# Seven block products for the first 1024 features of the last z2 projection

## The chip, the cores and the metric

The kernel is one program on 1 core of one Trainium2 chip. The metric is the device time of one execution in microseconds (us), with the inputs in HBM at the start and the output there at the end; several executions give a median. A core has five instruction streams that wait for each other only by semaphores. PE does matrix products from the on-chip memory SBUF into the accumulator memory PSUM, DVE and POOL do elementwise work, ACT does functions and scaled copies, and SP issues transfers (ACT and POOL issue some too).

## The reference, cut to what matters

```python
def reference(A_x, A_wqkv, A_wo, B_x, B_w_in, B_w_sp, B_b_sp, B_w_out):   # bf16, S = 2048, D = 1024, Fh = 1792
    x = A_x
    h = x + A(layernorm(x))        # attention, 32 heads, 8 keys at distance 2, then @ wo
    z = gelu(layernorm(h) @ w_in)  # 2048 x 3584, tanh form
    z1 = z[:, :Fh]
    z2 = layernorm(z[:, Fh:])      # over the 1792 features
    g = w_sp @ z2 + b_sp[:, None]  # over the 2048 tokens
    return h + (z1 * g) @ w_out
```

What the change touches is the product layernorm(h) @ w_in for the z2 half: the last 512 of the 2048 tokens, the first 1024 of the 1792 features.

## The kernel before

Tokens go through attention and the two projections in four chunks of 512 (CH), each of four tiles of 128. For a chunk, `head` multiplies by wo, adds x, stores h, takes the moments, normalises (`nrm`) and transposes each tile by a transfer that SP issues into hnT. `b_z2` then makes z2 with tokens as output rows, `b_z1` makes z1 with features as output rows. w_in lies in SBUF as four tiles: win0 and win1 for z2 (1024 and 768 columns), win2 and win3 for z1 (1024 and 768). After the last chunk a second phase multiplies by w_sp and w_out.

The last chunk (number 3) is treated apart. `b_z2(3)` is plain: for each tile 16 matmuls of 512 columns with win0, then 8 times 512 and 256 columns with win1, a gelu on ACT for each part, a square sum of 1792, statistics of that one tile, `nrm` on DVE and a store to HBM that POOL issues. `b_z1_blocks(3)` follows with seven block products (Strassen's form as Winograd has it): the 1024 long sum is cut in two halves, and so are the features and the tokens; sums of weight blocks (S, called form and win in the profile) and of token blocks (T, hnf) are formed on DVE in fp16, and seven products stand for eight. For range, the weights are scaled by a power of two, the level, which a chain over ACT, DVE and PE finds (`w1_level`: ACT takes absolute sums of win2 and win3). Its features come as three groups by blocks and two 128-feature pieces whole (`whole`, L1004) between the second group and the third.

A group of products uses two PSUM tiles of two banks, X and Y. X gets products 1, 7 and on top of them 2, 4; Y gets 5, 6 and on top 3:

```python
PRODS = (("k1", 1, 0), ("k4", 7, 0), ("k3", 5, 0), ("k2", 6, 0), ("k1", 2, 1), ("k4", 4, 1), ("k3", 3, 1))
```

ACT copies products 1, 7 and 5 into an SBUF tile of four slots (L1056, tile hb) before 2, 4 and 3 are added to their banks. DVE makes u = 6 + 1 (L1063), POOL w = 7 + 5 (L1064), DVE then c21, c22 and c12 in PSUM (L1065 to L1067), and ACT's gelu reads X and Y (L1083) and writes a tile of the pool xn, from which a transfer stores z1. PSUM tiles come from three slots "acc" of two banks; two more banks, "banka", opened at the end of attention, serve Y of the second group.

The order on each engine is fixed beforehand. All of this is recorded in an `Order`: each operation has an engine, an estimated time, what it depends on and how late, a priority, and slots that it takes or frees. `Order.run` then lists the operations in the order that a simple clock gives:

```python
def add(self, eng, us, fn, deps=(), prio=5.0, lat=0.1, take=None, free=None, table=None):
```

Each engine runs its list strictly in order, and an instruction that waits holds all behind it. Semaphores are set by the tile framework from the tiles that instructions read and write.

At the end of the stage the second phase begins: rows of w_sp (rawa, rawb) come by transposing transfers, DVE scales them by row (L1178) and makes their S forms (`t_forms`: L1190, L1196, L1192, L1194) and the z2 forms (`z_form`, L1214), PE runs `one_of` and `row_two` (L1279). z2 is loaded back from HBM by tokens: the halves (n, 0) of chunks 0 and 1, then (n, 1) of chunks 2 and 3 (L1205). `bias_rows` (L1168) multiplies a bias into the row scales, on DVE.

## Time and profile before

| | |
|---|---|
| median of 3 runs | 687.51 us (686.81 to 687.57) |
| profiled execution | 687.27 us |
| span of the profile | 685.5 us |
| PE busy | 679.0 us, 99% |
| DVE busy | 593.0 us, 87% |
| ACT busy | 357.6 us, 52% |
| POOL busy | 167.8 us, 24% |
| z2 of the last chunk on PE | 380.5 to 404.6 us |
| z1 of the last chunk on PE | 404.75 to 426.5 us |

The span runs from the first to the last instruction; the execution's own time has 1.8 us more around it. A line of a timeline gives start, length, engine, line of the kernel, operation, tiles out<-in and shape; in brackets is the idle time before it and what ended it. Lines of one kind that follow each other are joined, with their count at the end. Matmuls overlap, so a joined line of PE ends some 0.17 later than the next one starts. "Idle" counts only where nothing runs, so a wait on PE shows as a gap between lines.

### The profile page before, as it was taken

To read this page: it belongs to the slowest core of one execution; us is meant where nothing else is said; L and a number is where in the kernel's file an instruction comes from. 1 tells how busy PE (TensorE), PEld (TensorE's weight loads), DVE (VectorE), ACT (ScalarE), POOL (GpSimd) and SP (SyncE) were. 2 spreads that over 40 slices of the span, in tenths; PEclk is the share of its full clock that TensorE was granted. 3 is DMA by queue.
4 is the path that set the end of the run, shared out by engine and by line. 5 is a ranking of instruction groups with operands and counts; after the bars stand their busy time and mean duration, and the time that the engine had idled before them with its cause. 6 is when DMAs were issued, how large, how long until landed. Compare 5 with 4: busy or idle time off the path is not lost.

```text
span 685.5 us, 9209 instructions
## 1 busy us (share of the span) xinstructions
PE 679.0 (99%) x3424; PEld 360.4 (53%) x3441; DVE 593.0 (87%) x759; ACT 357.6 (52%) x530; POOL 167.8 (24%) x147
## 2 busy tenths in 40 slices
PE   9999999999999999999999999999999999999997
PEld 7766666566645445444544467444444444444443
DVE  6899899998999989999897868999799999755575
ACT  4547652353239998773883566388761122323131
POOL 0100010010210101000030124475461216553342
PEclk9999999999999999999999999999999999999999
DMA  8979579667995469444484996899957314642031
GB/s 319 335 242 248 169 192 280 154 160 262 226 350 226 93 239 238 163 176 118 111 220 135 199 295 186 284 285 317 275 184 190 123 53 132 185 123 93 1 122 63
DMA packets 144077, 133.07 MB, mean 194 GB/s; under 512 B 68768, under 2 KB 115776, under 8 KB 143904
## 3 DMA queue, kind: packets, MB, share of 16 engines
q1 hardware_dynamic: 132864, 88.93, 45.3%
q0 software_dynamic: 8416, 34.80, 17.9%
q10 hardware_dynamic: 2752, 8.75, 3.8%
q8 instruction: 27, 0.44, 0.3%
q14 instruction: 18, 0.15, 0.1%
HBM read 75.25 MB, written 33.10 MB: 158 GB/s over the span
## 4 chain that ended last, share of the span: by engine, by line
PE 99%; issue 0%; DVE 0%; ACT 0%; DVEq 0%
PE bank L1279 27%; PE acc L468 22%; PE acc L800 14%; PE acc L868 11%; PE banka L1279 10%; PE acc L723 8%; PE acc L1040 2%; PE acc L310 2%; PE wps L232 1%; PE acc L1004 1%; PE banka L1040 0%; PE L L562 0%; PE pb L624 0%; PE tpt L306 0%; ACT xnT L307 0%
## 5 line engine op out<-in xcount | busy, mean ns | idle before, releaser
L800 PE MATMUL acc<-win,hnT 128*128 128x512 bf16 (+1 forms) x501 | 97.4, 352 | 0.6
L800 PEld LDWEIGHTS <-hnT 128*128 128x128 bf16 x512 | 49.9, 98 | 47.4 <-issue 0.7
L532 DVE TENSOR_TENSOR prod<-qT,kT 128x4096 bf16<-128x4096 bf16 x32 | 72.7, 2282 | 1.6 <-ACT kT L474 1.3
L868 PE MATMUL acc<-hnT,win 128*128 128x512 bf16 x336 | 73.7, 379 | 0.0
L1279 PEld LDWEIGHTS <-zs 128*128 128x128 f16 x448 | 43.6, 98 | 52.8 <-DVE zs L1214 0.5
L479 ACT CAST stg<-acc 128x1024 bf16<-128x1024 f32 x36 | 36.4, 1011 | 61.9 <-PE acc L468 50.2
L468 PE MATMUL acc<-xnT,wk 128*128 128x512 bf16 x256 | 56.5, 379 | 0.0
L468 PE MATMUL acc<-xnT,wv 128*128 128x512 bf16 x256 | 56.4, 380 | 0.0
L723 PE MATMUL acc<-wo_sb,av_oT 128*128 128x512 bf16 x250 | 55.8, 379 | 0.3
L868 PEld LDWEIGHTS <-win 128*128 128x128 bf16 x336 | 32.7, 98 | 39.5 <-issue 0.7
L1279 PEld LDWEIGHTS <-z 128*128 128x128 bf16 x336 | 32.7, 98 | 39.1
L1279 PE MATMUL bank<-rawb,zs 128*128 128x512 f16 x224 | 52.6, 379 | 0.0
L1279 PE MATMUL banka<-rawa,z 128*128 128x512 f16 x224 | 51.9, 379 | 0.0
L1279 PE MATMUL bank<-form,zs 128*128 128x512 f16 x224 | 50.8, 379 | 0.0
L468 PEld LDWEIGHTS <-wk 128*128 128x128 bf16 x256 | 36.5, 143 | 19.0 <-issue 0.8
L468 PEld LDWEIGHTS <-wv 128*128 128x128 bf16 x256 | 36.5, 144 | 18.6 <-issue 0.5
L468 PE MATMUL acc<-xnT,wq 128*128 128x512 bf16 x192 | 41.9, 379 | 0.0
L723 PEld LDWEIGHTS <-av_oT 128*128 128x128 bf16 x256 | 24.9, 98 | 29.8
L807 ACT ACTIVATE u<-acc 128x1024 bf16<-128x1024 f32 (+1 forms) x32 | 29.2, 911 | 19.6 <-PE acc L800 19.4
L536 DVE TENSOR_TENSOR prod<-prod 128x2048 bf16<-128x2048 bf16 x32 | 38.7, 1216 | 0.0
L1279 PEld LDWEIGHTS <-sf 128*128 128x128 f16 x231 | 22.4, 98 | 26.3
L468 PEld LDWEIGHTS <-wq 128*128 128x128 bf16 x192 | 27.5, 143 | 13.9
(326 smaller groups left out, 1239.0 us busy)
## 6 DMA issues: line engine op xcount, KB each, us to landing
z<-z_d SPq DMA_DIRECT2D x28, 512.0 KB, 5.1
qkv_d<-stg SPq DMA_DIRECT2D x36, 256.0 KB, 4.7
wn<-in_B_w_sp_dram ACTq DMA_DIRECT2D x16, 512.0 KB, 5.5
z1c<-z_d SPq DMA_DIRECT2D x14, 512.0 KB, 4.8
z_d<-z1s SPq DMA_DIRECT2D x21, 256.0 KB, 2.8
z_d<-u SPq DMA_DIRECT2D x12, 448.0 KB, 2.5
av_y<-av_z POOLq DMA_DIRECT2D x4, 1024.0 KB, 9.8
av_oT<-av_zz POOLq DMA_DIRECT2D x4, 1024.0 KB, 15.3
```

The source lines that it names most:

```text
L232: T.matmul(wps[:], warm[:, 0:P], warm[:], start=True, stop=True)
L310: T.matmul(dst.rearrange("p (a b) -> p a b", b=P), wqs[:, kt, dl, :], xnT[0][:, lo:hi, kt, :], start=start, stop=stop)
L468: T.matmul(G[key][:, j, :].rearrange("p (a b) -> p a b", a=TPC), wv[:, kt, dl, :], xnT[c][:, :, kt, :], start=(kt == 0), stop=(kt == KT - 1))
L479: A.copy(stg[:], G[key][:])
L532: V.tensor_tensor(st["prod"][:], qT[:], kT[:, :, o:o + CH], op=ALU.mult)
L536: V.tensor_tensor(dst, p_[:, 0:4, :], p_[:, 4:8, :], op=ALU.add)
L723: T.matmul(st["acc", il][:, nh, :], oTs[c][:, dl, il * P:(il + 1) * P], wo_sb[:, dl, nh * CH:(nh + 1) * CH], start=(dl == 0), stop=(dl == ...
L800: T.matmul(accf[:, n0:n1], hnTs[c][:, il, kt, :], wins[hf][:, kt, n0:n1], start=(kt == 0), stop=(kt == KT - 1))
L807: A.activation(st["u", il][:, hf * 1024:hf * 1024 + wd], G["accz", c, il, hf][:].rearrange("p a b -> p (a b)")[:, 0:wd], ACTF.Gelu_apprx_t ...
L868: T.matmul(G["accy", c, fp][:, j, :].rearrange("p (a b) -> p a b", a=TPC), wt[:, kt, f0 * P:(f0 + 1) * P], hnTs[c][:, :, kt, :], start=(kt ...
L1040: T.matmul(d_, wt, mv, start=(not again and j == 0 and kt == 0), stop=(j == len(fps) - 1 and kt == 3), skip_group_check=bool(again))
L1279: T.matmul(dst, wts(k), mov(k), start=(first and k == 0), stop=(k == last - 1), skip_group_check=not first)
```

## The change

The z2 projection of the last chunk is made by `b_z2_blocks` in place of `b_z2`.

- The 768 columns of win1 stay whole (`late`), one tile after the other, ahead of the rest.
- The 1024 columns of win0 are made by seven products for each pair of tiles (0 and 2, 1 and 3), each of four matmuls of 512 columns. The order on PE is late 0, late 1, product 1 of both pairs, late 2, product 2 of both pairs, late 3, then 7, 5, 6, 4, 3 of the first pair and the same of the second. Y of the first pair uses the banka banks, all else acc tiles.
- The token forms are made once (`hn_forms`) and shared with z1. The weight forms of win0 are new: two of 2048 elements a partition, one in a tail behind win1 and one in place, and four of 1024 in xn tiles, with dependences that put them behind `nrm` or the moments of certain tiles.
- win0 is scaled on DVE, win2 and win3 now by 16 copies on ACT instead of four DVE operations. The level takes win0 into its sums, in 14 pieces of up to 1792, and is found during the last chunk's attention.
- The square sums are split in 768 and 1024, and the statistics of z2 are taken by pairs.
- In z1, Y of group 0 uses the banka banks instead of Y of group 1, and POOL makes its c22 into a zs tile. `bias_rows(0)` moves to POOL, the forms of the second phase change their order, and rawa is scaled tile by tile.
- On SP, the last z1 store of chunk 2 comes ahead of the h store of tile 2 and the transpose of that tile, and four z1 stores instead of three come ahead of chunk 2's transposes.

```diff
-                n_ = add("DVE", 0.5, nrm, [rs], prio=0.6)
+                n_ = G["normed2", il] = add("DVE", 0.5, nrm, [rs], prio=0.6)
+                G["moments2", il] = rs.deps[0][0]
...
+    def hn_forms(c):
+        ops, prev = {}, []
+        for m in (3, 1, 2, 4):
+            def f(m=m):
+                if "T" not in G:
+                    G["T"] = bp.tile([P, 4, 4, 2 * P], FP16, name="hnf", tag="hn%d" % ((c - 1) % 2), bufs=1)
...
+            prev = [add("DVE", 0.7, f, [G["hnT", c]] + prev, prio=2.65)]
+            ops[m] = prev[0]
+        return ops
+
+    def copies_tile():
+        if "copies" not in G:
+            G["copies"] = bp.tile([P, 4, CH], FP32, name="hb", tag="hb", bufs=1)
+        return G["copies"]
+
+    def b_z2_blocks(c, level):
+        st = {}
+        blk = lambda hk, j: w16(0)[:, 4 * hk:4 * hk + 4, j * CH:(j + 1) * CH]
+        scaled = []
+        for hk in range(2):
+            def sc(hk=hk):
+                half = wins[0][:, 4 * hk:4 * hk + 4, :]
+                V.tensor_scalar(half.bitcast(FP16), half, lev[:, 2:3], None, op0=ALU.mult)
+            scaled.append(add("DVE", 1.25, sc, [level, G["z2mm", c - 1, 0], G["avdone", c]], prio=2.6))
+
+        def s_half(m, h):
+            if m == 3:
+                return blk(0, 1)[:, 2 * h:2 * h + 2]
+            if m == 1:
+                return G["tail"].bitcast(FP16).rearrange("p (k n) -> p k n", k=4)[:, 2 * h:2 * h + 2]
+            if ("S", m, h) not in st:
+                st["S", m, h] = l1.tile([P, 2, CH], BF16, name="z1s", tag="xn", bufs=4)
+            return st["S", m, h][:].bitcast(FP16)
+
+        def s_w(m, h):
+            def f():
...
+            return f
+
+        sf_, prev = {}, []
+        for m, h in ((1, None), (3, None), (2, 0), (2, 1), (4, 0), (4, 1)):
+            behind = [] if h is None else [G["moments2" if h else "normed2", m // 2 - 1 + h]]
+            prev = [add("DVE", 1.22 if h is None else 0.7, s_w(m, h), scaled + behind + prev, prio=2.62, take="xn" if m in (2, 4) else None)]
+            sf_[m] = prev[0]
+        tf_ = G["tforms"] = hn_forms(c)
...
+        line = []
+
+        def late(il):
+            wd = win_specs[1][1]
+            deps = [G["hnT", c, il], G["win", 1]] + [(o, 0.0) for o in line[-1:]]
...
+                m_ = add("PE", 0.650, mm, deps, prio=order(), take="acc" if part == 0 else None)
+                deps = [(m_, 0.0)]
+            line.append(m_)
...
+            evs[il].append(add("ACT", 1.0, ev, [m_, G["z2st", c - 1, il]], prio=2.0, free="acc", lat=0.25, table="gelu"))
+            square(il, 1024, FH)
+
+        def bankof(a, b_):
+            nm = "XXYY"[b_]
+            if (nm, a) == ("Y", 0):
+                if (nm, a, b_) not in st:
+                    st[nm, a, b_] = zpools["ps"].tile([P, CH], FP32, name="banka", tag="banka", bufs=2)
+                return st[nm, a, b_][:]
+            if (nm, a) not in st:
+                st[nm, a] = new_acc()
+            return st[nm, a][:, b_ % 2, :]
+
+        def slot(a, n):
+            if n == 0:
+                if ("p1", a) not in st:
+                    st["p1", a] = zpools["z"].tile([P, CH], FP32, name="zs", tag="zs", bufs=5)
+                return st["p1", a][:]
+            return copies_tile()[:, n, :]
+
+        PR = {1: 0, 2: 0, 7: 1, 4: 1, 5: 2, 3: 2, 6: 3}
+        pe, cps = {}, {}
+        before = {}
+
+        def prod(p_, a):
+            def mm():
...
+            deps = scaled + [G["hnT", c, a + 2 if p_ == 3 else a]]
+            deps += [sf_[{3: 4, 5: 1, 6: 2, 7: 3}[p_]]] if p_ in (3, 5, 6, 7) else []
+            deps += [tf_[{7: 3, 5: 1, 6: 2, 4: 4}[p_]]] if p_ in (4, 5, 6, 7) else []
+            deps += [cps[{2: 1, 4: 7, 3: 5}[p_], a]] if p_ in (2, 3, 4) else []
+            deps += [G["close"]] + [(o, 0.0) for o in line[-1:]]
+            m_ = pe[p_, a] = add("PE", 0.864, mm, deps, prio=order(), take="acc" if p_ == 1 or (p_ == 5 and a == 1) else None)
+            line.append(m_)
+            if p_ in (1, 7, 5):
+                def cp():
+                    A.copy(slot(a, PR[p_]), bankof(a, PR[p_]))
+                cps[p_, a] = add("ACT", 0.6, cp, [m_] + ([G["hnT", c]] if a == 0 and p_ != 1 else []) + ([before[p_]] if a and p_ != 1 else []), prio=1.5, lat=0.15)
+
+        late(0)
+        late(1)
+        prod(1, 0)
+        prod(1, 1)
+        late(2)
+        prod(2, 0)
+        prod(2, 1)
+        late(3)
+        for a in range(2):
+            for p_ in (7, 5, 6, 4, 3):
+                prod(p_, a)
+
+            def dv(fn, deps, eng="DVE", us=0.7):
+                return add(eng, us, fn, deps, prio=2.0, lat=0.15)
+            u_ = dv(lambda a=a: V.tensor_tensor(slot(a, 3), bankof(a, 3), slot(a, 0), op=ALU.add), [pe[6, a], cps[1, a]] + ([before[7]] if a else []))
+            w_ = dv(lambda a=a: nc.gpsimd.tensor_tensor(slot(a, 1), slot(a, 1), slot(a, 2), op=ALU.add), [cps[7, a], cps[5, a]], eng="POOL", us=1.26)
+            c21 = dv(lambda a=a: V.tensor_tensor(bankof(a, 1), bankof(a, 1), slot(a, 3), op=ALU.add), [pe[4, a], u_])
+            c12 = dv(lambda a=a: V.tensor_tensor(bankof(a, 2), bankof(a, 2), slot(a, 3), op=ALU.add), [pe[3, a], u_])
+            if a == 0:
+                c22 = dv(lambda: nc.gpsimd.tensor_tensor(copies_tile()[:, 0, :], slot(0, 1), slot(0, 3), op=ALU.add), [u_, w_], eng="POOL", us=1.26)
+            else:
+                c22 = dv(lambda a=a: V.tensor_tensor(bankof(a, 3), slot(a, 1), slot(a, 3), op=ALU.add), [u_, w_, pe[3, a]])
+            before = {7: c22, 5: w_}
+            for il, nm, deps in ((a, "X", [pe[2, a], c21]), (a + 2, "Y", [c12, c22])):
+                halves = 2 if (nm, a) == ("Y", 0) else 1
+                for h_ in range(halves):
...
+                    evs[il].append(add("ACT", 1.22 if halves == 1 else 0.8, ev, [deps[h_]] if halves == 2 else deps, prio=1.9,
+                                       free="acc" if halves == 1 else None, lat=0.25, table="gelu"))
+                square(il, 0, 1024)
...
+            s0 = add("DVE", 0.32 if a else 0.48, st_tot, sqd[a] + sqd[a + 2], prio=0.5)
+            rs = batch_rstd(("l3", c, a), lambda cols=cols: st["stot"][:, cols], lambda cols=cols: st["sqs"][:, cols, 0],
+                            FH, f"l2_{a}", [s0], 0.5, cols=2)
+            for j in range(2):
...
+                n_ = add("DVE", 0.75, nrm, [rs], prio=0.6)
+                G["z2st", c, a + 2 * j] = dma_op(3.0, lambda: None, [n_])
+                G["z2n", c, a + 2 * j] = n_
 
...
-    W1CUTS = [(k, a) for k, n in ((2, 8), (3, 6)) for a in range(n)]
+    W1CUTS = [(k, a, min(a + FH, n)) for k, n in ((2, 8 * D), (3, 6 * D), (0, 8 * D)) for a in range(0, n, FH)]
...
         for k in (2, 3):
-            for hk in range(2):
-                def sc(k=k, hk=hk):
-                    half = wins[k][:, 4 * hk:4 * hk + 4, :]
-                    V.tensor_scalar(half.bitcast(FP16), half, lev[:, 2:3], None, op0=ALU.mult)
-                scaled[k, hk] = add("DVE", 1.5 if k == 2 else 1.15, sc, [level, last_mm[k], G["avdone", c]], prio=2.7)
-        hn = lambda hk, s2: hnTs[c][:, 2 * s2:2 * s2 + 2, 4 * hk:4 * hk + 4, :].rearrange("p il k s -> p k il s")
+            for kt in range(KT):
+                def sc(k=k, kt=kt):
+                    A.activation(w16(k)[:, kt, :], wins[k][:, kt, :], ACTF.Copy, scale=lev[:, 2:3])
+                scaled[k, kt // 4] = add("ACT", 1.06 if k == 2 else 0.81, sc, [level, last_mm[k]] + ([scaled[k, kt // 4]] if kt % 4 else []), prio=5.6)
...
-            prev = [add("DVE", 1.2, s_w(m, 2), [scaled[2, 0], scaled[2, 1], G["close"]] + prev, prio=2.8)]
+            behind = {1: G["normed2", 2], 3: G["moments2", 3], 2: G["normed2", 3], 4: G["normed2", 3]}[m]
+            prev = [add("DVE", 1.2, s_w(m, 2), [scaled[2, 0], scaled[2, 1], G["close"], behind] + prev, prio=2.8)]
...
-        before = {}
-        late = []
+        before = dict(G["copiesfree"])
+        before[1], before["c22"] = before[5], before[7]
...
-            if (nm, g) == ("Y", 1):
+            if (nm, g) == ("Y", 0):
...
-            c22 = dv("c22", lambda pt=pt, Y=Y: V.tensor_tensor(Y(1), pt(1), pt(3), op=ALU.add), [u_, w_, ops[3]])
+            if g == 0:
+                def apart(pt=pt):
+                    st["c22"] = zpools["z"].tile([P, CH], FP32, name="zs", tag="zs", bufs=5)
+                    nc.gpsimd.tensor_tensor(st["c22"][:], pt(1), pt(3), op=ALU.add)
+                c22 = dv("c22", apart, [u_, w_], eng="POOL", us=1.26)
+            else:
+                c22 = dv("c22", lambda pt=pt, Y=Y: V.tensor_tensor(Y(1), pt(1), pt(3), op=ALU.add), [u_, w_, ops[3]])
             c12 = dv("c12", lambda pt=pt, Y=Y: V.tensor_tensor(Y(0), Y(0), pt(3), op=ALU.add), [ops[3], u_])
...
-        V.tensor_tensor(wt_["rows"][:, cols], wt_["rows"][:, cols], wt_["b", pr], op=ALU.mult)
+        (V if pr else nc.gpsimd).tensor_tensor(wt_["rows"][:, cols], wt_["rows"][:, cols], wt_["b", pr], op=ALU.mult)
...
-    for c, r_ in ((0, r0_), (1, r1_)):
-        for k0 in range(0, NT, 4):
-            prev = [add("DVE", 1.2, lambda c=c, k0=k0: scale_raw(c, k0, 4), [r_, rl_] + prev, prio=3.5)]
-            if (c, k0) == (0, 4):
-                sc0 = prev[0]
+    for il, r_ in enumerate((ra_, rb_, r0_, r0_)):
+        prev = [add("DVE", 1.2, lambda il=il: scale_tile(0, il), [r_, rl_] + prev, prio=3.5)]
+    sc0 = prev[0]
+    for k0 in range(0, NT, 4):
+        prev = [add("DVE", 1.2, lambda k0=k0: scale_raw(1, k0, 4), [r1_] + prev, prio=3.5)]
     z_ld = {}
     for n in range(2):
         for hf in range(2):
             z_ld[n, hf] = dma_op(6.0, lambda n=n, hf=hf: load_z2f(n, hf), [r1_] + [G["z2st", 2 * hf + c, il] for c in range(2) for il in range(TPC)])
-    prev = [add("DVE", 0.7, lambda: bias_rows(0), prev, prio=3.55)]
+    add("POOL", 2.0, lambda: bias_rows(0), [rl_, G["hnT", NCH - 1]], prio=3.55)
     prev = [add("DVE", 0.7, lambda: z_form(0, 3), [z_ld[0, 0]] + prev, prio=3.55)]
-    for kind, n in (("z", 1), ("t", 0), ("t", 3), ("z", 2), ("z", 4), ("t", 1), ("t", 2)):
+    for kind, n in (("t", 0), ("z", 1), ("t", 3), ("z", 2), ("z", 4), ("t", 1), ("t", 2)):
```

183 lines of the change are left out of this document (121 added, 62 removed).

## The prediction

> **What bounds the kernel now.** I read the page first (busy time, then the chain that ended last), then the timelines of PE, ACT, DVE, POOL and SP's DMA queue between 370 and 445 us, where the changed stage lies, then the tile hnT.
>
> ```profile
> span 685.5 us, 9209 instructions
> PE 679.0 (99%) x3424; PEld 360.4 (53%) x3441; DVE 593.0 (87%) x759; ACT 357.6 (52%) x530; POOL 167.8 (24%) x147
> ...
> PE 99%; issue 0%; DVE 0%; ACT 0%; DVEq 0%
> ```
>
> PE is the bound, and the chain is all PE: a matmul less is its time less, and every wait put ahead of a matmul is time more. The PE timeline of the stage (start, length, line, tiles, count):
>
> ```profile
> 406.50 1.91 PE L1040 MATMUL acc<-hnf,form 128*128 128x256 f16 x16
> 408.24 1.04 PE L1040 MATMUL acc<-hnT,win 128*128 128x256 bf16 x8
> ...
> 416.98 3.62 PE L1004 MATMUL acc<-hnT,win 128*128 128x512 bf16 x16
> 420.43 1.04 PE L1040 MATMUL acc<-hnT,win 128*128 128x256 bf16 x8
> ...
> 440.36 1.89 PE L1279 MATMUL bank<-form,z 128*128 128x512 f16 x8
> ```
>
> Sixteen 512-column matmuls take 420.43 - 416.98 = 3.45 us, 0.216 each. A product of the block form takes four times that, 0.864 (eight of 256 columns in z1: 0.87). A group runs its products as 1, 7, 5, 6, 2, 4, 3; the first line holds 5 and 6, the second is 2. ACT copies 1, 7 and 5 out of PSUM:
>
> ```profile
> 406.69 1.07 ACT L1056 COPY hb<-acc 128x512 f32<-128x512 f32 x2 [0.85 <-PE acc L1040]
> 408.44 0.58 ACT L1056 COPY hb<-acc 128x512 f32<-128x512 f32 x1 [0.67 <-PE acc L1040]
> ...
> 413.77 0.60 ACT L1056 COPY hb<-banka 128x512 f32<-128x512 f32 x1
> 414.24 1.14 ACT L1083 ACTIVATE z1s<-acc,wlim 128x1024 bf16<-128x1024 f32 x1
> ...
> 422.38 1.07 ACT L1056 COPY hb<-acc 128x512 f32<-128x512 f32 x2 [0.49 <-PE acc L1040]
> ```
>
> The copies of 1 and 7 begin 0.19 after 7 ended (406.50), not after 1: two banks in one acc tile are waited for together. So does the copy of 5, 0.20 after 6 ended (408.24). The first pair is done at 407.76, product 2 begins at 408.24: 0.48 to spare, 0.42 behind the 0.06 of a semaphore. The third group: 423.45 against 423.92. The sum u that follows is DVE's:
>
> ```profile
> 409.06 0.69 DVE L1063 TENSOR_TENSOR hb<-acc,hb 128x512 f32<-128x512 f32 x1 [2.94 <-ACT hb L1056]
> ...
> 425.35 1.25 DVE L1214 TENSOR_TENSOR zs<-z,z 128x1024 f16<-128x1024 bf16 x1
> ...
> 436.63 2.29 DVE L1194 TENSOR_TENSOR form<-rawa,form 128x4096 f16<-128x4096 f16 x1
> ```
>
> ```profile
> 424.79 1.26 POOL L1064 TENSOR_TENSOR hb<-hb 128x512 f32<-128x512 f32 x1 [1.91 <-ACT hb L1056]
> ...
> 437.82 2.22 POOL L1523 TENSOR_TENSOR p<-p,p 128x512 f32<-128x512 f32 x1 [5.17 <-ACT p L1489]
> ```
>
> A DVE sum of two SBUF tiles takes 0.69 alone; begun inside a POOL sum it ends 0.55 after that (426.60 against 426.05). A POOL sum begun inside a DVE one (437.82) grows from 1.26 to 2.22 instead. Whichever starts first runs, the other waits. Last, the transposes of the tokens:
>
> ```profile
> 381.93 0.37 SPq L876 DMA_DIRECT2D z_d<-z1s  x1
> ...
> 386.67 1.26 SPq L752 DMA_TRANSPOSE hnT<-hb  x1
> ```
>
> ```profile
> L800 PE MATMUL acc<-win,hnT x126: 272/379/379, 380.5 to 404.6; 128*128 128x512 bf16 x94, 128*128 128x256 bf16 x32
> ...
> DMA to landing us min/median/max: 3.1/3.7/4.4
> ```
>
> The fourth transpose is issued at 386.67 and lands at 390.8. PE first needs that tile at 398.7: eight us of cover.
>
> **The change part by part.** Times are this profile's; the stage begins at 380.54 on PE.
>
> *Matmuls.* 64 of 512 columns become 56: 8 x 0.216 = **-1.73**. The 768-column part is the same work.
>
> *Fourth token tile.* PE now needs it after three whole tiles (2.59 each) and four products: 380.54 + 7.78 + 3.46 = 391.78, seven us sooner. Its transpose waits for nrm of tile 3, which on DVE now stands behind the last S form of win0 and a form of win2. That S form takes the xn buffer that the z1 store of 381.93 reads; the store lands in 4.0, at 385.9. Then 0.1 + 0.6 (pitch of a 1024 form) + 1.13 (2048 form) + 0.54 (nrm) + 0.1: issue at 388.4, landing after 3.1 to 4.4, that is 391.5 to 392.8. Wait 0 to 1.0; I take the 4.14 that this transpose took: **+0.75**.
>
> *Products of the second pair (tiles 1 and 3).* The order is 7, 5, 6, 4, 3, and 5 and 6 share an acc tile that 3 writes. From the end of 6: 0.20, the copy 0.62, u 0.69, 0.06 = 1.57 until 3 may start. One product (0.864) stands between, not two as in z1: **+0.70**. Pair one has its own bank for each, and no wait. Bounds 0 (copies by bank) to 0.8.
>
> *ACT order in z1.* In group 0 a gelu of the second pair now stands between the copies of 1 and 7, in group 2 a gelu of z1. Each has a pitch of 1.02 against 0.42 to spare: **+0.60 twice**. Bounds 0 and 1.0: the gelu's whole pitch, if the cover is gone.
>
> *Whole features after group 1.* Their acc tile comes free with group 0's gelu. Before it ACT now runs the copy of 5 and a square of 1024 (1.05 + 0.19, pitch about 1.08, by Abs): from the end of 6, 0.20 + 0.49 + 1.08 + 1.12 + 0.06 = 2.95 against three products, 2.6: **+0.35**, from 0 to 0.6.
>
> *Forms for the next stage (DVE).* Before, the last of them ends at 438.92 for the matmul at 440.36. After u of group 2 a rawb scaling (1.22, two SBUF inputs) replaces a form of 0.69, +0.52, and two more z forms follow, 1.2 together. That exceeds the 1.38 to spare by 0.35, but the +0.60 in group 2 falls behind u, ahead of the consumer, and covers it. What decides is L1523: before it started 1.2 after this form; now the form starts some 0.1 after the POOL sum would, and then waits for it: 0 or 0.95, **+0.5** as I can't place 0.1. Were the memory's bandwidth shared, both orders would stretch the form, and the sum would take 0.95; but its row of 2.29 beside POOL is not stretched. The Trainium skill, page "SBUF — State Buffer", section "SBUF: two separate sides", calls it an exclusive lock of the port pair of DVE and POOL, held by whichever starts first; by it the sum below is +1.3 or +2.3, never between, and the trace's two orders agree. Its "Perfetto Trace Analysis", section "Optimizing Scalar/DVE Operations", says that moving work between those two might not help; for the bias rows below, that is a warning against the move.
>
> *At nothing.* Bias rows to POOL: no POOL row of 128x1024 16-bit exists; 1.26 (its 512 float sum) to 2.5. Begun just ahead of the token forms it holds them up to 1.8, but they have the 2.59 of the fourth whole tile as cover. W sums and c22 on POOL: DVE's combining reads PSUM and isn't held. Level sums of 8192 more elements a partition, 8.5 us of ACT in attention 3: ACT idles more than that there and PE waits for none of it. Scaling win2 and win3, moved from DVE (4.6 us) to ACT (16 copies, about 15 us by L1419's 2.00 for 2048): behind the gelus they end near 399.5, the forms of win3 follow, and u of the second pair still comes later by its copy than by them. Scaling and forms of win0 (7.6 us of DVE) fill DVE's idle time from 374 to 391. SP: the z1(2) store goes ahead of h_d and the third transpose, which lands about 387 for 387.5; the extra store ahead of hnT(2)'s transposes costs 1.7 us of some 3 to spare. Statistics by pairs: z2 lands later, next paragraph.
>
> *Sum.* -1.73 + 0.75 + 0.70 + 1.20 + 0.35 + 0.5 = **+1.8**. The profiled execution took 687.27 (685.5 of span, 1.8 around it) and so becomes 689.1. It lies 0.24 below the median of the three runs, 687.51: **689.3**.
>
> **Rivals.**
> - *By bank.* If a copy went by its own bank, products 2 and 3 would not wait: terms 0.70 and 1.20 go, and the rest is 0 or so, 687.4: not slower. It decides if copies start at the end of 1 and 5. Against it: 406.69 and 408.44 above. Shorter landings end in the same place (the fourth tile at 3.1 and no POOL lock take 1.25 off, 688.0).
> - *Full gain.* All waits hidden, -1.73: 685.8. PE at 99% speaks for it, and so does the skill's "Perfetto Trace Analysis", section "Identifying Performance Opportunities": improve the most-contended engine. By it the sum would stop at the first term. Against it: the margins of 0.42 on which the old order ran.
> - *z2 late.* The last two z2 tiles are normed together at about 419 and stored by 420.5, two issues of 0.6 to 0.75 on. Before, such stores took 2.8 to 7.3 and the second pair of loads 4.7 and 6.0, landing at 421 and 423 for matmuls at 430.0 and 431.7, which the sum moves 1.3 later. Now the loads land at 428 to 432.6 and 429.7 to 434.3 for 431.3 and 433.0. The middle fits; the far end costs 1.3 more: 690.6.
>
> **How the numbers follow.** Forecast 0.54 (688.4 to 690.2 by its own bounds), by bank or shorter landings 0.26, full gain 0.10, z2 late 0.10. Two tenths of a per cent, 1.4 us, is about what a measurement tells from no change: 686.1 to 688.9. Full gain is the only case faster: 0.10. Slower: z2 late and four fifths of the forecast, 0.10 + 0.43 = 0.53. Same: the rest, 0.37. The range leaves out the full gain and ends a little outside the others: 687.0 to 690.9.
>
> **What would show it.** 56 matmuls and the 1.73; PE idle ahead of the fourth tile's first matmul, released by a hnT transpose issued near 388.4; ahead of product 3 of the second pair, released by DVE's u; ahead of product 2 of groups 0 and 2, released by an ACT copy with a gelu before it; ahead of the whole features; and at the matmul of L1194's form, with that form at 3.3 if the lock took it. Without these idles the forecast is wrong and the time is near 686; with an idle at the second z2 load it is above 690.

## The result, and the profile after

| | before | after |
|---|---|---|
| median | 687.52 us (6 runs, 686.81 to 687.78) | 691.28 us (6 runs, 691.12 to 691.41) |
| ratio to before, 95% interval | | 1.0056 [1.0043, 1.0069] |
| span of the profile | 685.5 us | 689.6 us |
| weight loads on PE | 3441 | 3433 |

The change makes the kernel slower by 3.8 us. The forecast was 689.3, the range 687.0 to 690.9: the sign was right, the time lies above the range. Busy time and the chain that ended last, from the page of the changed kernel:

```profile
PE 679.0 (98%) x3417; PEld 359.4 (52%) x3433; DVE 600.3 (87%) x761; ACT 381.7 (55%) x562; POOL 173.8 (25%) x150
...
PE 93%; DMA 3%; DVE 1%; POOL 1%; ACT 1%; issue 1%; SPq 0%; DVEq 0%; ACTq 0%
```

Eight weight loads fewer are eight matmuls fewer. The chain, all PE before, now leaves PE for transfers, DVE, POOL and ACT. Where, the timeline of PE in the changed kernel says:

```profile
388.19 2.77 PE L942 MATMUL acc<-win,hnT 128*128 128x512 bf16 x15 [0.17 <-DMA hnT<-hb]
390.80 1.89 PE L985 MATMUL acc<-win,hnT 128*128 128x512 f16 x8
393.55 2.77 PE L942 MATMUL acc<-win,hnT 128*128 128x512 bf16 x16 [0.86 <-DMA hnT<-hb]
...
404.75 1.02 PE L985 MATMUL acc<-z1s,hnT 128*128 128x512 f16 x4 [0.66 <-DVE hb L1012]
...
409.83 1.03 PE L1232 MATMUL acc<-hnT,win 128*128 128x256 bf16 x8 [0.57 <-ACT hb L1246]
...
418.93 3.61 PE L1196 MATMUL acc<-hnT,win 128*128 128x512 bf16 x16 [0.20 <-ACT z1s L1279]
...
426.60 1.03 PE L1232 MATMUL acc<-hnT,win 128*128 128x256 bf16 x8 [0.56 <-ACT hb L1246]
...
433.07 1.90 PE L1480 MATMUL banka<-rawa,z 128*128 128x512 f16 x8 [0.24 <-DMA z<-z_d]
435.88 1.47 PE L1480 MATMUL banka<-rawa,z 128*128 128x512 f16 x6 [0.91 <-DMA z<-z_d]
```

The last two lines lie in the first row of matmuls on z2. Before, PE ran that row without a gap:

```profile
426.54 7.07 PE L1279 MATMUL banka<-rawa,z 128*128 128x512 f16 x32
```

What a wait costs is the start of a line less the start that the line before it would have allowed. Between the second line (390.80, eight matmuls at 0.216) and the third (393.55) that is 393.55 - 390.80 - 1.73 = 1.02; the bracket shows 0.16 less, because the tail of the last matmul counts as busy. Read in this way the eight gaps are:

| place | gap | the prediction's term |
|---|---|---|
| third token tile, 388.19 | 0.33 | 0 (lands about 387 for 387.5) |
| fourth token tile, 393.55 | 1.02 | 0.75 |
| product 3 of the second pair, 404.75 | 0.81 | 0.70 |
| product 2 of z1's group 0, 409.83 | 0.73 | 0.60 |
| whole features, 418.93 | 0.37 | 0.35 |
| product 2 of group 2, 426.60 | 0.74 | 0.60 |
| second z2 loads, 433.07 and 435.88 | 0.39 + 1.07 | a rival: 1.3, at 0.10 |
| t2 form behind POOL's sum | 0 | 0.5 |

They add to 5.46. The stage itself begins at 380.93 for 380.54: 0.14 of these 0.39 are there at 10 us already, long before the change (10.31 for 10.17), and some 0.2 lie at the first z2 matmul of chunk 2 (317.35 for 317.00, less the 0.14). So 0.14 + 0.2 + 5.46 - 1.73 = 4.1, the difference of the two spans. To 0.1 the gaps account for the whole difference; what is left is why.

### The profile page after: what moved, and what is told of

The parts are those of the page before. It is cut to its first block, busy times and chain, and to the rows that moved or that the text cites. A ratio compares the mean times of both kernels' runs of the same rounds, so it can differ in the third digit from the quotient of the medians.

```text
span 689.6 us, 9238 instructions
## 1 busy us (share of the span) xinstructions
PE 679.0 (98%) x3417; PEld 359.4 (52%) x3433; DVE 600.3 (87%) x761; ACT 381.7 (55%) x562; POOL 173.8 (25%) x150
## 4 chain that ended last, share of the span: by engine, by line
PE 93%; DMA 3%; DVE 1%; POOL 1%; ACT 1%; issue 1%; SPq 0%; DVEq 0%; ACTq 0%
PE bank L1480 27%; PE acc L468 22%; PE acc L802 11%; PE acc L1071 10%; PE banka L1480 9%; PE acc L723 8%; PE acc L310 2%; DMA z<-z_d 1%; PE acc L985 1%; DMA hnT<-hb 1%; PE wps L232 1%; DMA z_d<-u 1%; DMA z_d<-z1s 1%; PE acc L1232 1%; PE acc L942 0%
## 5 line engine op out<-in xcount | busy, mean ns | idle before, releaser
L802 PE MATMUL acc<-win,hnT 128*128 128x512 bf16 (+1 forms) x375 | 73.2, 352 | 0.5
L802 PEld LDWEIGHTS <-hnT 128*128 128x128 bf16 x384 | 37.3, 98 | 35.5 <-DMA hnT<-hb 0.5
L1324 ACT ACTIVATE wn<-wn 128x1024 bf16<-128x1024 bf16 x32 | 33.5, 1055 | 0.0
```

The costliest lines, as they stand in the source:

```text
L802: T.matmul(accf[:, n0:n1], hnTs[c][:, il, kt, :], wins[hf][:, kt, n0:n1], start=(kt == 0), stop=(kt == KT - 1))
L1324: A.activation(h_, h_, ACTF.Abs, accum_out=wabs[:, i, hf:hf + 1])
```

## The experiments

Each kernel is the changed one with the edit shown. Times are medians; each was run against the kernel before on one chip, whose medians were 687.32 to 687.47. The gaps are those of the one profiled execution, and executions of one kernel spread by up to 1.8 us (edit 2: 689.93 to 691.76): the profiled one is the shortest in edits 3 and 4 and the longest in 5, 12 and 14. So gaps say where the time is, and only the medians say how much. All fourteen:

| edit | median | ratio to before, 95% | gaps on PE that are left |
|---|---|---|---|
| 1 product 3 moved | 690.47 | 1.0046 [1.0031, 1.0061] | 0.42, 1.08, 0.51, 0.72, 0.73, 1.22 |
| 2 copies told of the banks | 690.64 | 1.0047 [1.0031, 1.0064] | 0.42, 0.73, 0.81, 0.66, 2.30 |
| 3 nrm of tile 3 first | 690.67 | 1.0050 [1.0035, 1.0065] | 0.18, 0.58, 0.82, 0.74, 0.36, 0.74, 0.42, 0.93 |
| 4 other z2 rows read | 690.91 | 1.0052 [1.0037, 1.0067] | 0.86, 0.82, 0.73, 0.36, 0.73, 0.93, 0.33 |
| 5 one z1 store back | 690.70 | 1.0047 [1.0031, 1.0064] | 0.29, 0.90, 0.82, 0.74, 0.37, 0.74, 0.55, 0.85, 0.40 |
| 6 z2 loads cut, sum p on DVE | 690.04 | 1.0039 [1.0024, 1.0054] | 0.20, 0.88, 0.81, 0.74, 0.37, 0.74, 0.88 |
| 7 edits 1, 2, 3, 5 | 690.64 | 1.0048 [1.0033, 1.0062] | 1.50, 0.51, 0.74, 2.06 |
| 8 edits 6 and 7 | 688.70 | 1.0020 [1.0011, 1.0030] | 1.37, 0.51, 0.73, 0.81 |
| 9 nrm of tile 3 out of place | 689.73 | 1.0032 [1.0020, 1.0044] | 0.81, 0.74, 0.37, 0.74, 0.68, 0.55 |
| 10 all of these | 687.69 | 1.0007 [0.9998, 1.0016] | 0.22, 0.77, 1.25 |
| 11 sum p back in place | 687.42 | 1.0000 [0.9991, 1.0008] | 0.48, 0.24, 0.37, 0.77 |
| 12 z2 stores from SP | 686.85 | 0.9991 [0.9982, 1.0001] | 1.93, 0.68 |
| 13 early z2 loads ahead | 686.25 | 0.9984 [0.9975, 0.9993] | 0.21, 0.38, 0.68 |
| 14 as 13, ACT and DVE waits left | 689.36 | 1.0030 [1.0018, 1.0042] | 0.28, 0.82, 0.73, 0.37, 0.74, 0.94, 0.32, 0.40 |

### 1 to 4: one cause each

**1. Product 3.** Product 3 of the first pair goes between 6 and 4 of the second, so that u has two products of cover.

```diff
-            for p_ in (7, 5, 6, 4, 3):
+            for p_ in (7, 5, 6, 4) if a == 0 else (7, 5, 6):
                 prod(p_, a)
+            if a == 1:
+                prod(3, 0)
...
+                prod(4, 1)
+                prod(3, 1)
```

> Product 3 of the first pair is moved between 6 and 4 of the second, so that two products stand between 6 and 3 there. Theory 'each wait adds': PE's wait of 0.82 us ahead of the second pair's product 3 goes, and 691.28 becomes about 690.5; if the gelus of the second pair come earlier as well, up to 0.7 less at group 0. Rival 'one chain takes all' (a wait that goes is taken up by the next, as the z2 stores set the end): 691.1 to 691.4. Rival 'DVE is simply late there': the wait stays at 0.8 and moves to product 4.

The wait of 0.81 is gone; product 4 waits 0.51 instead, for the copy of 7, which ACT now runs behind that of 5. The gaps of group 0 and of the whole features went too, one of 0.72 came at product 1 of group 2, which waits for a gelu to free its PSUM tile, and the median fell by the 0.8 that the first theory gave. So the mechanism is the one that the sum names; what the repair frees in one place comes back in part in another.

**2. The planner is told what the semaphores do.** The copies of 1 and 5 depend on products 7 and 6 of the same tile, so that the list puts the gelus ahead of them.

```diff
+                if p_ == 7 or p_ == 6 and g != 0:
+                    ops["cp", {7: 1, 6: 5}[p_]].deps.append((ops[p_], ops[p_].lat))
                 if p_ in (1, 7, 5):
```

> The planner is told what the semaphores do: in z1 the copy of product 1 waits for 7, and the copy of 5 for 6 where they share a tile. The gelus then stand ahead of the pair of copies in groups 0 and 2, and the last square of z2 ahead of group 1's copies. Theory 'each wait adds': the waits of 0.73 at groups 0 and 2 and of 0.37 at the whole features go, and with the earlier square some or all of the 1.48 ahead of the second z2 loads: 688.0 to 689.5. Rival 'one chain takes all': 691. If only the two gelus matter and z2's lateness has another cause (slow loads): 689.5 to 689.9.

Group 0's 0.73 and the whole features' 0.37 went. In group 2 the gelu does run ahead of the copies now, but it waits 0.53 for a z1 store to free its buffer, so 0.66 of the gap stays. PE reached the second phase earlier and stood there, as its timeline shows:

```profile
433.53 3.84 PE L1482 MATMUL banka<-rawa,z 128*128 128x512 f16 x16 [2.14 <-DMA z<-z_d]
```

2.30 instead of 1.46: most of the 1.10 was given back to the z2 loads. These are not one more wait in the row; they end a chain of their own, which gains only when the last statistics are earlier. The median, 690.64, lies between what the first theory gave (up to 689.9) and the second's 691.

**3. nrm of tile 3 ahead of the last forms on DVE.**

```diff
-            behind = [] if h is None else [G["moments2" if h else "normed2", m // 2 - 1 + h]]
+            behind = [] if h is None else [G["normed2", 3] if (m, h) == (4, 1) else G["moments2" if h else "normed2", m // 2 - 1 + h]]
...
-            behind = {1: G["normed2", 2], 3: G["moments2", 3], 2: G["normed2", 3], 4: G["normed2", 3]}[m]
+            behind = {1: G["normed2", 2], 3: G["normed2", 3], 2: G["normed2", 3], 4: G["normed2", 3]}[m]
```

> DVE normalises tile 3 ahead of the win0 form that waits for a z1 store and of a win2 form. Theory 'each wait adds': PE's 1.02 us ahead of the fourth tile goes: 690.3. Rival 'the transposes are slow by crowding': the transpose is issued two us sooner but lands late all the same, over half of the wait stays: 690.8 or more. Rival 'one chain takes all': 691.2.

The fourth tile's gap fell from 1.02 to 0.58 only. DVE and POOL of this kernel:

```profile
386.85 1.20 DVE L747 TENSOR_SCALAR hb<-hb,l_3nmean,l_3rstd 128x1024 bf16<-128x1024 bf16 x1 [2.46 <-DMA h_d<-hb]
```

```profile
385.65 2.12 POOL L1364 TENSOR_TENSOR rows<-rows,brow 128x1024 bf16<-128x1024 bf16 x1 [0.63 <-ACT win L1136]
```

First in line, nrm still waits 2.46, for the store of h: nrm works in place on hb, and the store, issued at 382.64, landed 4.1 later. In the changed kernel nrm began at 388.03, after that store had landed (issued at 382.78, 4.1 too), so there DVE's order was the last thing it waited for, as the prediction had it; the store is the next bound, close behind. And nrm takes 1.20 for 0.54 beside POOL's bias rows, which end at 387.77, and ends 0.28 after them. The median fell by 0.6: of z2's 1.46 only 0.42 is left, but 0.93 came at the z form of the next features.

**4. Other z2 rows.** The second z2 loads read the first half of the token rows again, which were stored long before; the product with w_sp then leaves out the rows of chunks 2 and 3.

```diff
-        dma(t[:], z2_view[:, hf * HK:(hf + 1) * HK, 2 * i * P:(2 * i + 2) * P])
+        dma(t[:], z2_view[:, 0:HK, 2 * i * P:(2 * i + 2) * P])
```

> The second z2 loads read the first half's rows (tokens 0 to 1023) again, so that they wait for no late store; the spatial product then uses the wrong half of z2. Theory 'the last z2 stores are late': the waits of 0.40 and 1.08 us ahead of row_two go: 689.8. Rival 'the loads themselves are slow, at whatever time': they stay at 8 us, but are issued 10 us sooner, so PE's wait goes as well, and the trace tells by their length. Rival 'the DVE forms are as late as the loads': 0.5 us of it comes back at the forms: 690.3.

Both gaps at the z2 loads vanish, so it is the last stores that the loads wait for. But 0.93 appears at the t2 form, and the median fell by 0.37 only, to 690.91, for 689.8 expected (690.3 by the nearest rival). DVE and POOL of this kernel:

```profile
439.57 3.27 DVE L1390 TENSOR_TENSOR form<-rawa,form 128x4096 f16<-128x4096 f16 x1
```

```profile
439.43 1.26 POOL L1721 TENSOR_TENSOR p<-p,p 128x512 f32<-128x512 f32 x1 [4.99 <-ACT p L1687]
```

POOL's sum starts 0.14 before the form, runs its 1.26, and the form takes 3.27 for 2.29. This is the term that the prediction could not place between 0 and 0.95; in the changed kernel PE's lateness hides it (POOL's sum starts at 442.00 there, DVE's form at 440.64).

### 5 to 8: chunk 2's store, the z2 loads, and everything together

**5. One of the four z1 stores goes back behind chunk 2's transposes.**

```diff
+            def store(fp=fp):
...
+            s_ = G["z1store", c, fp] = dma_op(0.01, store, [(e_, -0.93)] + ([(G["hnT", 2], -7.9)] if c == 1 and fp in (3,) else []))
+            dma_op(3.0, lambda: None, [s_, e_], free="xn")
```

> One part undone: in chunk 2's z2, one of the four z1 stores ahead of the transposes of hnT(2) on SP goes behind them, as it was before. The prediction costed the four stores at nothing (1.7 us of some 3 to spare); the changed kernel's profile shows the first z2 matmul of chunk 2 at 317.35 behind a gap of 0.19, against 317.00 behind 0.10. If the SP queue is the cause, the transposes are issued near 306.8 instead of 308.69, the gap there is 0.10, and everything after is some 0.35 earlier: about 690.9, with the z2 loads taking none of it back, since they come earlier by the same amount. Rival: that 0.35 lies in attention's matmuls, which do not wait for these transposes; then the time stays at 691.3.

The transposes are issued at 307.27 and no longer at 308.69; chunk 2's z2 then starts 306.81 after the first long row of matmuls at 10 us, against 307.04 in the changed kernel and 306.83 before. The extra store cost 0.23, not 0, and other kernels bear it out: 306.98 to 307.04 in those without this edit (306.84 in edit 4 apart), 306.79 to 306.86 in those with it. The median fell by 0.58, more than this; what the rest is isn't shown, as the profiled execution is the longest of this kernel.

**6. The z2 loads cut by chunk, POOL's first sum p on DVE.**

```diff
+    for n in range(2):
+        z_ld[n, 2] = dma_op(3.0, lambda n=n: load_z2f(n, 1, 0, TPC), [r1_, z_ld[1, 0]] + [G["z2st", 2, il] for il in range(TPC)])
+    for n in range(2):
+        z_ld[n, 1] = dma_op(4.5, lambda n=n: load_z2f(n, 1, TPC, HK), [z_ld[1, 2]] + [G["z2st", 3, il] for il in range(TPC)])
...
-            nc.gpsimd.tensor_tensor(p7[:], p7[:], p5[:], op=ALU.add)
+            (nc.gpsimd if n else V).tensor_tensor(p7[:], p7[:], p5[:], op=ALU.add)
```

> The late z2 loads are cut in two by token chunk, so that what waits for the last stores (issued 423.07) is 0.25 MB and not 0.5 MB, with the rest loaded ahead; and the first POOL sum p of the second phase (L1721) runs on DVE behind the forms, so that it can't hold the t2 form. Theory: the time sits in the landings and behind them in the lock: the 0.39 and 1.07 at the second z2 loads go to 0.4 or less together, and the 0.93 that appeared at the t2 form when half of the rows was left unread does not come in their place: 689.6 to 690.2. Rival: the loads' landing is set by the stores ahead of them and by the other traffic, not by their size; then the z2 gaps stay at 1.0 or more and the time is above 690.7. A second rival is that DVE, with 0.69 more ahead of the next z forms, is late for the first matmul of the second features: a gap of 0.3 to 0.9 at 455.

Both gaps go, z2's and the t2 form's; DVE is late for the next features instead (0.88), as the second rival said. But edits 3 and 9, whose sum p stays on POOL, have such a gap too (0.93 and 0.55), so the 0.69 that DVE took over isn't its only cause; edit 11 has another. The median falls by 1.2.

**7. Edits 1, 2, 3 and 5 together,** with one more z1 store moved behind the third transpose of chunk 3:

```diff
+    G["z1store", NCH - 2, NF // 2 - 1].deps.append((G["hnT", NCH - 1, 2], -3.9))
```

> The four single repairs together: product 3 of the first pair moved into the second pair's products, the planner told that two banks of one tile are waited for together, nrm of tile 3 ahead of the win0 and win2 forms, and the z1 stores behind the transposes of chunks 2 and 3. The z2 loads are left as they are. If the waits add, what each took (0.33 + 1.02 to some 0.6, 0.81 to 0.5, 0.73, 0.37, 0.35) sums to about 2.7 less and the time is 688.6. If the second z2 loads are a chain of their own, from the last statistics over stores of 4.3 and loads of 7 to 8, most of that is taken back ahead of the second phase: a gap of 2 to 3 there, and 689.8 to 690.6.

The waits of the third tile, of chunk 2, of group 0 and of the whole features are gone, product 4 waits 0.51 where product 3 waited 0.81, and 0.74 stays in group 2; yet the time is that of edit 2 alone. Two places took it. PE's timeline at the second phase:

```profile
433.18 3.63 PE L1493 MATMUL banka<-rawa,z 128*128 128x512 f16 x16 [1.90 <-DMA z<-z_d]
```

2.06 here, and 1.50 at the fourth tile, where nrm stands behind the h store and the bias rows. The second theory holds: the chain over HBM takes it back.

**8. Edits 6 and 7 together.**

> The four repairs together with the z2 loads cut in two by chunk and the first sum p on DVE. If the eight matmuls' 1.73 was all there to be had and only waits took it, this one keeps about 1 of it: 0.4 to 1.0 of waits left at the fourth tile and product 4, 686.5 to 687.6, at or below the kernel before (687.4). If the z2 chain over HBM is the limit whatever the size of the load, it stays at 689 to 690 with a gap of 1.5 or more ahead of row_two.

688.70: 1.9 below edit 7, which leaves the z2 chain, and 1.3 below edit 6, which leaves the waits. With the z2 chain shortened, the waits of the stage do come off. It did not reach the kernel before, since four gaps were left, 3.42 in all, and these are the ones to take away next.

### 9 to 11: the four that were left

Kernel 9 stands alone on the change; from 10 to 13 each kernel has the edits of the one before it.

**9. nrm of tile 3 out of place.** It writes into the tile's own xr, so that the h store no longer matters, and its transpose goes ahead of rawa's on SP (edit 3 is in it).

```diff
+                    to = st["xr", il][:] if il == 3 else st["hnc"][:, il, :]
+                    V.tensor_scalar(to, st["hnc"][:, il, :], t["nmean"][:], t["rstd"][:],
...
-    ra_ = dma_op(4.0, lambda: load_raw(0, 0, 1), [G["close"], rl_.deps[0], (G["hnT", NCH - 1, 2], 0.0 - 3.9)])
+    ra_ = dma_op(2.5, lambda: load_raw(0, 0, 1), [G["close"], rl_.deps[0], (G["hnT", NCH - 1, 3], 0.0 - 3.9)])
```

> One cause alone, the fourth token tile. nrm of tile 3 writes into the xr tile of its own instead of hb in place, stands ahead of the last win0 form on DVE, and its transpose goes ahead of the first rawa transpose on SP. Moving nrm alone (the third kernel of these) won 0.44 of the 1.02, since nrm then waited for the h store of 382.6, which reads hb and landed 4.1 later. If that store was what held it, nrm now runs at about 385.3, the transpose is issued by 386.2 and lands by 390.9, ahead of the 391.8 at which PE wants the tile: the gap at the fourth tile goes to 0.1 or less. The whole stage then is 0.9 to 1.0 earlier, the z2 stores with it: 690.2 to 690.4. Rival: the transposes share their engines with the rawa transposes and stores, and the landing grows by what the issue gains (as the 11.0 of the longest one shows it can); then a gap of 0.4 or more stays. A second rival is that the z2 loads at the end don't move with the stage, and their gaps grow from 1.46 to over 2: no gain in the time.

DVE and SP's queue of this kernel:

```profile
385.01 0.55 DVE L748 TENSOR_SCALAR xr<-hb,l_3nmean,l_3rstd 128x1024 bf16<-128x1024 bf16 x1 [0.66 <-POOL l_3rstd L692]
```

```profile
385.58 1.23 SPq L755 DMA_TRANSPOSE hnT<-xr  x1
```

Issued at 385.58 instead of 388.60, the transpose has landed when PE wants it: no gap at the third or fourth tile. The median falls by 1.55, to 689.73 for the 690.2 to 690.4 expected, the largest step of any single repair. The z2 gaps shrink with it (0.68 for 1.46). That the stage comes earlier doesn't explain this: the loads are issued 1.5 earlier (425.92 for 427.39), and PE wants them 1.5 earlier too. What went is the gap at the second load, which lands sooner after its issue; why is not shown. A gap of 0.55 comes at the next features.

**10. All repairs,** with the copy of 7 ahead of that of 5 in the second pair, the gelu of the second z1 group's Y behind the copy of 7 of the third, and POOL's first sum p put behind the two that follow it.

```diff
+                cps[p_, a] = add("ACT", 0.6, cp, [m_] + ([cps[7, a]] if (p_, a) == (5, 1) else []) + ([G["hnT", c]] if a == 0 and p_ != 1 else []) + ([before[p_]] if a and p_ != 1 else []), prio=1.5, lat=0.15)
...
+            if g == 2:
+                e_.deps.append((ops["cp", 7], 0.0))
...
+            if not n:
+                nc.gpsimd.tensor_tensor(p7[:], p7[:], p5[:], op=ALU.add)
```

> All repairs so far (the four, and the z2 loads cut by chunk), with the four waits that the best of them had left (1.37 at the fourth tile, 0.51 at product 4 of the second pair, 0.73 in the last group of z1, 0.81 in the second phase) taken away at their causes: nrm of tile 3 out of place and its transpose ahead of rawa's; the copy of 7 of the second pair ahead of that of 5; the gelu of the second group's Y behind the copy of 7 of the third; and the first POOL sum p back on POOL, but behind the two sums that follow it, so that neither the t2 form nor DVE pays for it. If the waits are all there is between the eight matmuls' 1.73 and the measured +3.8, this is 1.2 to 1.7 faster than the kernel before: 685.7 to 686.2. If the waits only move on (z2 loads, the next landing), it stays at 687.3 or above.

Between 381 and 430 us PE waits only 0.22; the time is that of the kernel before. Left are 0.77 at the z2 loads and 1.25 that I had made. DVE and POOL there:

```profile
449.77 3.10 DVE L1425 TENSOR_TENSOR zs<-z 128x1024 f16<-128x1024 bf16 x1
```

```profile
449.94 1.28 POOL L1741 TENSOR_TENSOR p<-p,p 128x512 f32<-128x512 f32 x1
451.16 1.16 POOL L1784 TENSOR_TENSOR rows<-u,rows 128x512 f32<-128x512 f32 x1
```

A DVE form of 0.68 took 3.10 beside two POOL sums back to back and ended 0.55 after the second, although its row starts 0.17 ahead of the first. The sum that was moved (445.13) is not one of the two; they are the next features' p and the sum behind it, and moving the other had shifted what POOL runs next to this form. In edit 11 they start at 449.44 and 451.96, and no longer back to back.

**11. The sum p back where the change has it.**

> The kernel of all repairs (687.69, with 0.77 ahead of the last z2 rows and 1.25 in the second phase), with the first POOL sum p put back where the change has it. That sum starts some 2.5 ahead of the matmul that wants the t2 form (437.82 against 440.36 in the kernel before); with the waits of the stage gone the t2 form is on DVE from 436.6, ahead of 437.1, so the form has the port and the sum stretches. Theory: the lock's loss was an effect of the late stage, and moving the sum only pushed POOL's next two sums onto the z form of 449.8, which took 3.10 for 0.68. Then 1.25 goes and nothing comes at the t2 form: 686.3 to 686.8, below the kernel before (687.47). Rival: the form loses the race by a little, 0.9 at the t2 form: 687.3 or more.

The t2 form, on DVE from 436.67, is ahead of the sum of 437.09 and takes 2.29; POOL's sum stretches to 3.00 instead. That part of the theory holds. But the gap of 1.25 becomes 0.77, not 0. PE waits there for the z form of 451.80 on DVE, and ahead of that form stands a product of two SBUF tiles:

```profile
448.49 2.78 DVE L1828 TENSOR_TENSOR zg<-zg,z1c 128x1024 f16<-128x1024 f16 x1
```

```profile
449.44 1.28 POOL L1740 TENSOR_TENSOR p<-p,p 128x512 f32<-128x512 f32 x1
```

It takes 0.69 in edit 10, where POOL had nothing beside it, and 2.78 here, and it ends 0.55 after POOL's sum p of the next features, as the DVE sums held by POOL do (426.60 for 426.05 in the prediction). So the lock is the likely cause of this gap too. Every kernel but edit 10 has this row with 2.76 to 2.78, the kernel before included; there the z form ends at 452.41 for a matmul at 452.46, so a PE that comes earlier must wait. This is read from the times: no run moved this one sum, and the product's row starts 0.95 ahead of the sum's, with two issues of transfers on POOL in between, so what holds it until the sum begins stays open. And 0.48 stands at product 3 of the second pair, which waits for the copy of 5. The median is 0.3 lower, for the 0.9 to 1.4 expected, and the intervals of the two kernels overlap.

### 12 to 14: what was still open, z2's way over HBM

**12. The four z2 stores of the last chunk from SP's queue instead of POOL's.**

```diff
-                    dma_w(z2_d[i * P:(i + 1) * P, :], st["u", il][:])
...
+                def z2_out(il=a + 2 * j):
+                    i = c * TPC + il
+                    dma(z2_d[i * P:(i + 1) * P, :], st["u", il][:])
...
+                G["z2st", c, a + 2 * j] = dma_op(3.0, z2_out, [n_])
```

> As the last one, and the four z2 stores of the last chunk go out from SP's queue (as those of chunks 0 to 2 do) and not from POOL's, where three z1 stores, a reciprocal root and a sum stand around them (last z2 store at 420.13, second norm done by 419.7). If the order of POOL's queue is what is left of the late z2, the last store goes out 0.4 to 0.8 earlier, lands some 0.5 to 1 earlier, and the 0.77 ahead of the last rows falls to 0.3 or less: 685.7 to 686.3. If the landing of stores and loads (4.2 and 5.3) is what is left, the gap stays near 0.7 and the time with it.

The median is 686.85, for the 685.7 to 686.3 expected if POOL's queue was what was left, and the interval still holds no gain at all. Executions spread from 686.17 to 687.65, five of the eleven at 686.42 or below; the profiled one, the longest, has a gap of 1.93. The issue of the last two stores takes 1.12 and 1.45 us, behind chunk 2's loads, where the first two took 0.33 each. SP's queue in it:

```profile
415.17 0.99 SPq L1063 DMA_DIRECT2D z_d<-u  x2
416.21 1.80 SPq L1417 DMA_DIRECT2D z<-z_d  x2
418.13 2.68 SPq L1063 DMA_DIRECT2D z_d<-u  x2
426.18 1.98 SPq L1417 DMA_DIRECT2D z<-z_d  x2
```

**13. The chunk 2 parts of the z2 rows issued ahead of all four stores.**

```diff
-        z_ld[n, 2] = dma_op(3.0, lambda n=n: load_z2f(n, 1, 0, TPC), [r1_, z_ld[1, 0]] + [G["z2st", 2, il] for il in range(TPC)])
+        z_ld[n, 2] = dma_op(3.0, lambda n=n: load_z2f(n, 1, 0, TPC), [r1_] + [G["z2st", 2, il] for il in range(TPC)])
```

> As the last one, but on SP's queue the chunk 2 parts of the z2 rows (two loads of 0.25 MB, which depend on nothing of the last chunk) are issued right behind the first two loads at 407 and no longer between the stores of the two pairs. If a queue serves in order, the last two stores (issued 418.1 to 420.8, landing by 426.2, 5.4 to 6.0) land 1.5 to 2.5 sooner, the gap of 1.93 ahead of the last rows goes to 0.3 or less, DVE's z form no longer waits (1.65), and with it most of the 0.68 in the second phase: 685.3 to 686.0, 0.2% or more below the kernel before (687.32). If the landing is set by the traffic of z1 stores and rows as such, the gap stays at 0.8 or more and the time at 686.6 or above.

SP's queue:

```profile
405.94 3.70 SPq L1417 DMA_DIRECT2D z<-z_d  x4
415.21 3.81 SPq L1063 DMA_DIRECT2D z_d<-u  x4
423.82 0.92 SPq L1417 DMA_DIRECT2D z<-z_d  x2
```

The last store's issue ends at 419.02 instead of 420.81 and it has landed by 423.82 instead of 426.18. The gap falls from 1.93 to 0.38 in the profiled executions, the median by 0.6 only, to 686.25: ratio 0.9984 [0.9975, 0.9993], just below the kernel before. The intervals of 12 and 13 overlap, and five executions of 12 were as short as 13's; so the step from 12 is likely and not shown. Of the 2.36 that the last loads gain, 1.8 lie in the issue of the stores and 0.6 in their landing. The Trainium skill, page "DMA: Bandwidth & Descriptors", section "Queues, rings and completion order", says that each engine consumes the descriptors of a ring in order; the two kernels are in line with it (landing 5.4 behind two loads, 4.8 without), though 0.6 from one execution each is little. In the second phase 0.68 is left, where I had expected most of it to go; the DVE product of edit 11 stands ahead of the late z form again (447.67, 2.77 long).

**14. As 13, but with the waits of ACT and DVE left in:** edits 3, 9 and the z2 chain of 13, without edits 1, 2, 5 and those of 10.

> The change with the fourth token tile early and the z2 chain of the last kernel, and nothing done on the waits of ACT and DVE (0.81 at product 3, 0.74 and 0.74 at product 2 of z1's first and third group, 0.37 at the whole features: 2.66 in all). If waits add, this one is 2.3 to 2.7 above the last kernel, some 688.0 to 688.6, with no gap at the z2 loads. If the stage were bound by something else once z2 comes in time (DVE's forms behind it), the two would differ by 1.5 or less, and a gap at the t2 form or at 455 would make up for it.

689.36, that is 3.1 above 13, more than the 2.3 to 2.7 expected. The four waits are there with 0.82, 0.73, 0.74 and 0.37, 2.66 in all, and z2 makes no gap. The largest of the rest, 0.94, is the t2 form again, where DVE shows:

```profile
439.45 3.27 DVE L1392 TENSOR_TENSOR form<-rawa,form 128x4096 f16<-128x4096 f16 x1
```

With 0.28 at the third tile, 0.32 and 0.40 in the second phase and 0.2 at chunk 2 the gaps add to 4.8, 3.5 more than the 1.27 of edit 13; the spans of the two profiled executions differ by 3.9, of which 0.36 lies in the start of the program. The waits add, once z2 is not late; with z2 late, part of them was free.

## Why the prediction was right in its sign and wrong in its time

The frame was right: PE is the bound, a matmul is its time, and the order around the copies is what the change upsets. Step by step:

- *Matmuls, -1.73.* Right: eight weight loads fewer. Edit 13, in which gaps of 1.27 are left, takes 300.22 from the start of the stage to the last matmul, and the kernel before 300.66: 0.44 less, which is 1.73 less 1.27. So the gain is there to be had. Of the 1.1 between the two spans another 0.32 lie ahead of the stage and 0.34 behind the last matmul.
- *Fourth token tile, +0.75.* Right mechanism, 1.02 measured. The issue was named to 0.2 (388.4; 388.60), the landing took 4.90, above the 4.4 that bounded it: 0.27 too little. nrm was late behind DVE's order, as it says; what it left out is the next bound, the h store that reads hb (edit 3), and with that out of the way too the wait was gone (edit 9).
- *Product 3, +0.70; copies behind a gelu, +0.60 twice; whole features, +0.35.* Right: 0.81, 0.73, 0.74 and 0.37, each released by the instruction named. The first three were mis-sized by 0.11 to 0.14; that a copy waits for both banks of its tile, which decided against the rival "by bank", held in every run that left the order alone.
- *POOL's lock on the t2 form, +0.5.* A figure between the two ends does not occur: it is 0 in the changed kernel, 0.93 and 0.94 in kernels whose z2 came in time and whose sum was left in place (edits 4 and 14). Which of the two it was hung on the z2 loads: their lateness held PE, and so the sum, until the form had begun. The Trainium skill's "SBUF: two separate sides" in "SBUF — State Buffer" (held by whoever starts first, for the whole instruction) agrees with 2.29 that became 3.27, and with the POOL sum that became 3.00 where DVE was first. Two DVE rows that start ahead of POOL's sum (by 0.17 in edit 10, by 0.95 in edit 11) and yet end 0.55 after it do not fit that, by the starts that the trace records; who is first is not always read from the starts.
- *At nothing, the third tile and the store ahead of chunk 2's transposes.* Wrong: 0.33 and some 0.2. The third tile's transpose was issued at 383.29 and fed PE 4.9 later, above the 4.4 again. "Some 3 to spare" for the latter was not there; 1.4 later was enough to be seen (edit 5).
- *z2 late, a rival at 0.10 priced +1.3.* This is the step that failed: the chain from the last norm over the stores to the second loads was left out of the sum and priced only as a case of its own, in which nothing else goes wrong. It happened, on top of everything in the sum, with 1.46. That 1.46 is close to the 1.3 is luck. The 1.3 is a second load that lands at 434.3 for a matmul due at 433.0; it fed PE at 435.88 for one due at 434.80, so both were off by more than the gap. Edit 4 bounds what the step was worth alone: with z2 read in time the median fell to 690.91 only, since 0.93 came at the t2 form in its place, still at the end of the range. The rest is what was set at nothing and the sizes below.

Where the chain ran late can be read step by step. The prediction lets the last norm end at 419 and the stores go by 420.5 and two issues. DVE and POOL of the changed kernel have

```profile
421.30 1.47 DVE L1052 TENSOR_SCALAR u<-u,l_1nmean,l_1rstd 128x1792 bf16<-128x1792 bf16 x2 [0.35 <-POOL l_1rstd L692]
```

```profile
419.75 0.77 POOL L1283 DMA_DIRECT2D z_d<-z1s  x1
420.54 0.73 POOL L692 TENSOR_TENSOR l_1rstd<-l_1var,nhalf 128x2 f32<-128x2 f32 x1
421.22 1.13 POOL L1283 DMA_DIRECT2D z_d<-z1s  x1
422.35 0.55 POOL L1054 DMA_DIRECT2D z_d<-u  x1
423.07 0.55 POOL L1054 DMA_DIRECT2D z_d<-u  x1 [0.17 <-issue]
```

The last norms end at 422.77, and the last store goes out at 423.07, behind its norm. Two waits of 0.9 in this can be named. The square sum of the pair was there at 417.77, but its statistics began at 418.68, since DVE's norms of the first pair took 2.36 beside a POOL sum (1.40 in edits 10 and 11, without it). The variance was there at 419.63, but the reciprocal root began at 420.54, behind the issue of a z1 store. The issue of the next z1 store held the first z2 store by up to 0.3 more. The loads were issued at 427.39, 4.3 after the last store began; the first landed 5.6 later, for 4.7 before, and the second fed PE some 8.0 after its issue at 427.8. The prediction reckons with 6.0 for that one, a figure that no row of the trace shows: the landing of that load is not among them, before or after. Every term of the sum delayed this chain as well as PE, so setting it against matmuls "1.3 later" left "the middle fits"; but the chain goes through POOL's and DVE's queues too, and these were not followed.

Added up, the miss of 2.3 in the span is 1.46 - 0.5 for z2 and the lock, 0.33 and 0.2 for what was set at nothing, 0.67 for sizes (0.27, 0.11, 0.13, 0.14, 0.02) and 0.14 for the start of the program. The range failed in the same place: it priced "z2 late" alone, at 690.6, and let no case have it together with terms at their upper ends.

Open stays what is left in edit 13: 0.68 in the second phase, where DVE's z form comes late. Ahead of it stands the product that takes 2.77 for 0.69 and ends 0.55 after a POOL sum; a kernel with that sum out of its way alone was not tried.
